# v held in two halves of 64 partitions, and another order of the instruction streams, in a packed attention with a gated convolution

## The chip, the core and the metric

The kernel runs on one core of a Trainium2 chip. TensorE (PE) multiplies matrices into PSUM; its weight loads are shown apart as PEld. VectorE (DVE), ScalarE (ACT) and GpSimd (POOL) work on tiles, and SyncE (SP) issues the DMAs. The metric is the device time of one execution in microseconds (us). All arithmetic is on 32-bit floats.

## The reference

Eight batches, eight heads, 576 tokens, 64 channels a head, 32 packed queries p a head. The packed queries attend to the tokens; then the tokens attend to the packed result. The heads side by side give x, which goes through a causal convolution of five taps for a gate, a value product and an output product.

```python
def sm_attn(qq, kk, vv):
    s = scale * np.matmul(qq, kk.transpose(0, 1, 3, 2))
    s = s - np.max(s, axis=-1, keepdims=True)
    a = np.exp(s)
    a = a / (np.sum(a, axis=-1, keepdims=True) + 1e-09)
    return np.matmul(a, vv)
p_packed = sm_attn(p, k, v)
out = sm_attn(q, p_packed, p_packed)

gate = 1.0 / (1.0 + np.exp(-gate_pre))   # gate_pre: five taps of conv_w over x
val = x @ w_val
return (gate * val @ w_out).astype(np.float32)
```

## The kernel before

The work of a batch is cut into steps, each a Python generator that yields after a few instructions. `ORDER` is a string of tokens: a letter for the step, the batch, and how many pieces of it to emit now. `run` takes the tokens in turn, and `InOrder` ties each instruction to the one before it on its engine. So the string alone sets the order on all five engines.

The letters: K, V, Q, P load k, v, q, p; L and J load the weights of the value and output products, and C, W, N turn them from 64-bit floats, which come as pairs of words, into 32-bit ones. k and q turn k and q so that channels lie on partitions: batches 0 and 1 by TensorE (`turned`, TURNED), the others by VectorE's transpose of 32x32 blocks. a is the attention of the packed queries: scores s1 into the PSUM tile `quad`, of which there is one; a maximum (nb); Exp into a1; transposes of a1 in pieces of 128 columns (at) and ScalarE copies (a1t); the product pv with v. p and c prepare the packed result. s and t are the attention of the tokens, its softmax with the sums on VectorE, and a2 with its high part a2h and its rest a2l. g is the gate, half a batch at a time, also in `quad`; w and v (the small letter) make the value product in three parts of lower precision and multiply it with the gate into gvh and gvl; o is the output product, one chunk of 128 tokens at a time, copied into one of two `osb` buffers and stored. H is an idle turn: four transposes of the identity that nobody reads.

A head's 576 tokens lie as nine to a partition (NE = 9): a partition holds tokens 9w to 9w+8 of one head. Two heads of a group of partitions share a tile, so v of a batch is two tiles of 128 partitions, 64 partitions to a head of each pair (G = 2). In `attn_pack` the transposes take, for each e of nine, the 64 columns of both groups together; pv multiplies, for each e and group, 64 rows of a1t by 64 rows of v for each of four heads.

SP issues loads in the order of the string, and a load waits until its buffer is free. k and q share five buffers ("m"), v has four.

Of the kernel before, what the change touches and what calls it, by code (L numbers as in the profile page):

```python
# [15 lines left out]


NB = {
    "words": 4, "top": 1, "vtop": 4, "p": 1, "m": 5, "a1": 1, "v": 4, "xT": 4, "pT": 1, "a1t": 1, "pp3": 1, "ppk": 1, "t2": 3, "a2h": 3, "a2l": 3,
    "wp": 3, "sig": 3,  # L20
}

# [6 lines left out]


ORDER = """
J0 L0.2 C0.4 P0 C0 K0 N0 K0 C0.2 N0.2 C0 W0 L0 W0 Q0 W0 N0 k0.7 W0 N0 W0 N0.2 W0 H0 W0.2 k0.2 Q0 k0 W0 k0 C0 k0 L0
k0 W0 q0 k0.2 W0 N0 a0.2 q0 V0 q0 W0 C0 q0 N0 a0.2 W0.2 H0 L0 V0 a0 W0.3 a0.7 q0 C0 q0 W0 J0 q0 W0 N0 a0 W0.2 N0.2
q0.3 a0 p0 N0 q0 p0 q0 W0 N0 W0 s0 N0 s0 W0 K1.2 s0.3 k1 N0 k1 P2 k1 V1 k1 Q1 k1.5 H0 k1 s0 H0 s0 t0 k1 c0 k1 q1.2
Q1 s0 q1 k2 q1 t0.2 a1 q1 H0 a1 s0 K2 J0 q1 H0 t0.3 H0.2 a1.2 q1.4 t0.3 w0 q1 k2.2 a1 q1 t0 J0 W0 t0 W0 t0 c0 a1 K3
N0.2 a1 w0.2 a1 K2 a1 g0 N0.3 k2 W0 N0.3 a1 V1 v0 g0 v0 a1 a2 Q2.2 a2 a1 N0.4 a2 a1 a2 a1 a2 K3 a2 p1 k3 p1 k3 a2 s1
N0.2 V2 N0 a2 s1 W0 | s1 V2 v0.2 V3 N0.4 v0.2 a2 k3.2 v0 g0 P4 V4 v0 g0 v0 s1 a2 v0 s1 q2 a2.2 a3.2 K4 s1 a2 t1 s1
v0 N0 V3 a3 t1 a2 p2 Q3 a3 o0 k4 k5 v0 p2 t1 o0.2 a3 q2 t1.2 s1 t1 s1 t1 k4 t1 o0 p2 o0 a3 p2 K4 v0 a3 c1 s2 a3 v0
t1 s2.3 t1.2 c1 t1 v0 a3 s2 K5 w1 g1 w1 s2 w1 g1 v1 s2 a3.2 g1 t2 v1 k4 v1 v0 k4 s2 Q3 o0 a3 v1 s2 g1 v1 a4 v1.2 k5
a3 a4 t2.3 a4.2 a3 t2 v1 o0 v1 V4 o0 q3 K5 q3 a4 p3 a4 p3 o1 v1.5 t2 o1 a4 p3.2 K6 w2 a4 o0 t2.2 k5 s3.2 Q4 c2 a4.2  # L40
t2 s3 t2 o1 w2 o1 a4 t2.2 s3 w2 P6 c2 g2 k5 g2 v2 a5 o1 v1 a4 a5 o0 a5.2 v2 a5 k6 v2 o0 s3 a4 s3 v1 Q4 v2 q4 a5 o1
V5 a5 s3 t3 a5.3 t3 a4 g2 q4 t3 V5 p4.2 t3 p4 v2 k6 K6 Q5 s3.2 p4 v2 o1 v2 g2 o0 a5 s4 a5 v2 s4 v2 s4.2 o1 v2 s4 v2
k6 V7 Q5 o2 k6 t3 a5 o2 o1 Q6 t3.2 c3.2 t3 a6 k7 o1 a5 s4 a6.3 p5 v2 k7 o1 v2 t3 o2.2 t3 q5 a6.2 K7 a6 v2 t3 v2 t3
V6 o2 w3.2 p5 s4 g3.2 w3 o1 a6 t4 s4.2 v3.4 Q6 t4.2 p5 g3 a6 p5 o2 v2 q5 g3 o2.3 q6 v3 a6 v3.2 o1 v3 t4 v3 V6 o3 v3
t4.2 o1.2 c4 v3.3 a6 k7 a6 s5 v3 s5 t4 o3.2 s5 c4 a6 o2 t4 o3 s5.2 a6 w4 o2 t4.4 w4 g4 o3 p6 w4 o3 q6 g4 p6 s5 v4 p6
v4 g4 v4 g4 K7 v4 s5 k7 V7 v3 s5 p6 v3 v4.2 t5.2 o2 t5 o3 s6.2 Q7 t5 v4 t5 v4 s6 o3 s6 v4 o3 v4 s6.3 o3 a7 s6 v4 a7
o4 v4 o3.2 t6 a7.2 t5 s5 o4 s6 v4 a7 t5 a7 Q7 o4.2 c5 t5 v4 o4 t5.2 a7 c5 t5.2 w5.2 g5 w5 a7 v5 a7 g5.2 a7 g5 v5 a7
t6.5 c6 a7 v5.3 v4 o3 v5.2 v4 v5.2 o5 v5.2 a7 o3 o4 c6 t6.2 o4 o3 a7 q7.2 v5 t6 p7 o5 p7.2 o4 v5 p7 o5 s7.2 o4 s7.2
t6 s7.3 t6 o5 v5 o4 o5 t7 t6 w6.3 g6.2 v6 g6 v5 v6.2 o5 o4 v5 v6 t7 s7 t7 s7 v6.2 t7 v6 t7.3 o5 o4 o5 v6 g6 v6 c7
v6.3 o6 v6.2 t7 o5.2 t7 o6 t7.3 o5 c7 g7.2 w7 o6 g7 w7.2 o5 g7 v7.2 v6 v7 o5.2 v7 o6.2 v7 v6 v7 o7 v7.2 o7 v7.4 o5  # L50
o6.4 v7 o7 v7.3 o7.27 o6 H0 o6.2
"""


# [25 lines left out]
def packed_attention_gated_conv(  # L80
# [8 lines left out]
    w_out: bass.AP,  # L89
    out: bass.AP,  # L90
):

# [86 lines left out]
            st["p", b + n] = t[:, n]  # L181
        yield

    def load(b, nm, src, tag="m"):
        rows = src[b].rearrange("h s d -> (h s d)").rearrange("(h a x) -> a h x", h=4, a=P)
        for n in range(2):
            m = st[nm, b, n] = tile_of(tag, [P, 2, NE, D], F32, f"{nm}m_{b}_{n}")
            sp.dma_start(m.rearrange("a h e d -> a h (e d)"), rows[:, 2 * n : 2 * n + 2])
            yield

# [1 line left out]
        yield from load(b, "k", k)  # L192

    def load_v(b):
        yield from load(b, "v", v, "v")

    def load_q(b):
        yield from load(b, "q", q)
# [140 lines left out]
    def keys(b):  # L339
        if b in TURNED["k"]:  # L340
            if b % 2 == 0:
                pd = tile_of("osb", [P, 4, 2 * D], F32, f"pd_{b}")
                act.mul(
                    pd.rearrange("a h (u d) -> a h u d", u=2),
                    st["p", b].unsqueeze(2).broadcast_to([P, 4, 2, D]),
                    scale,
                )
                yield
                pt = one(f"pTt_{b}").rearrange("a (h x) -> a h x", x=P)
                for hl in range(4):  # L350
                    pe.transpose(pt[:, hl], pd[:, hl], ident)
                yield
                pT = tile_of("pT", [P, 4, P], F32, f"pT_{b}")
                for n in range(2):
                    st["pT", b + n] = pT.rearrange("a h (g n j) -> a h g n j", g=G, n=2)[:, :, :, n]
                act.copy(pT, pt)
                yield
            yield from turned(b, "k")
            return
        t = st["p", b]  # L360
        pT = st["pT", b] = tile_of("pT", [P, 4, 2, NP], F32, f"pT_{b}")
        act.mul(t, t, scale)
        yield
        dve.transpose(pT.rearrange("a h c z -> a (h c z)"), t.rearrange("a h d -> a (h d)"))
        yield
        yield from channels(b, "k")

    def channels(b, nm):
        for n in range(2):
            xT = st[f"{nm}T", b, n] = tile_of("xT", [P, 2, NE, D], F32, f"{nm}T_{b}_{n}")  # L370
            dve.transpose(
                xT.rearrange("a h e d -> a (h e d)"),
                st[nm, b, n].rearrange("a h e d -> a (h e d)"),
            )
            yield

    def queries(b):
        if b in TURNED["q"]:
            yield from turned(b, "q")
            return  # L380
        yield from channels(b, "q")

    def scores(name, b, pT, nm):

# [14 lines left out]
    def scores_turned(name, b, pT, nm):  # L399


        s = quad(name)[:, :, :HS]
        for g in range(G):
            for par in range(2):
                rows = slice(D * par, D * par + D)
                for hl in range(4):
                    to = s[heads[hl], 2 * g + par, : 2 * P]
                    xT = st[f"{nm}T", b, hl // 2][rows, hl % 2, :NE4, NW * g : NW * g + NW]
                    pe.matmul(
                        to.rearrange("a (e w) -> a e w", w=NW), pT(g, hl)[rows], xT, start=True, stop=True  # L410
                    )
        for t in range(NQ):
            for hl in range(4):
                xT = st[f"{nm}T", b, hl // 2][:, hl % 2, NE4, NP * t : NP * t + NP]
                pe.matmul(
                    s[heads[hl], t, 2 * P : 2 * P + NP], pT(t // 2, hl), xT, start=True, stop=True
                )
        return s

    def attn_pack(b):  # L420
# [3 lines left out]
        else:  # L424
            s1 = scores(f"s1_{b}", b, lambda rows, c, hl: pT[rows, hl, c], "k")
        yield
        a1 = tile_of("a1", [P, NE, G, NW], F32, f"a1_{b}")
        parts = 2 if b in TURNED["k"] else 1
        sums = tile_of("sm1", [P, 2, G], F32, f"sm1_{b}")
        rs = sums[:, 0]  # L430
        for g in range(G):
            x = s1[:, 2 * g : 2 * g + 2]
            nb = tile_of("nb1", [P, 1], F32, f"nb1_{b}_{g}")
            dve.tensor_reduce(nb, x, axis=AX.XY, op=ALU.max, negate=True)
            yield
            if b in TURNED["k"]:
                pairs = (
                    (
                        a1[:, : 2 * NE4, g].rearrange("a (e t) w -> a t e w", t=2),
                        x[:, :, : 2 * P].rearrange("a t (e w) -> a t e w", w=NW),  # L440
                    ),
                    (a1[:, 2 * NE4, g].rearrange("a (t z) -> a t z", t=2), x[:, :, 2 * P :]),
                )
            else:
                pairs = (
                    (
                        a1[:, :, g].rearrange("a e (t z) -> a t e z", t=2),
                        x.rearrange("a t (e z) -> a t e z", z=NP),
                    ),
                )  # L450
            for n, (to, of) in enumerate(pairs):
                act.activation(to, of, AF.Exp, bias=nb, accum_out=sums[:, n, g : g + 1])
            yield
        if b in TURNED["k"]:
            dve.scalar_tensor_tensor(rs, rs, 1e-9, sums[:, 1], op0=ALU.add, op1=ALU.add)
        else:
            dve.tensor_scalar_add(rs, rs, 1e-9)
        dve.reciprocal(rs, rs)
        yield
        a1t = tile_of("a1t", [P, NE, P], F32, f"a1t_{b}")  # L460
        for n in range(0, NE, NE4):
            es = range(n, min(n + NE4, NE))
            at = one(f"at_{b}_{n}").rearrange("a (e y) -> a e y", y=P)
            for e in es:
                pe.transpose(at[:, e - n], a1[:, e].rearrange("a g w -> a (g w)"), ident)
            yield
            act.copy(a1t[:, n : n + len(es)], at[:, : len(es)])
            yield
        pv = big(f"pv_{b}")[:, :, :D]
        for e in range(NE):  # L470
            for g in range(G):
                rows = slice(NW * g, NW * g + NW)
                for hl in range(4):
                    pe.matmul(
                        pv[heads[hl], g],
                        a1t[rows, e, heads[hl]],
                        st["v", b, hl // 2][rows, hl % 2, e],
                        start=(e == 0),
                        stop=(e == NE - 1),
                    )  # L480
        yield
        if b in TURNED["q"]:
            pp3 = st["pp3", b] = tile_of("pp3", [P, G, 2, D], F32, f"pp3_{b}")
# [286 lines left out]
```

## Time and profile before

| what | us |
|---|---|
| median of 3 runs | 312.02 |
| the runs | 312.02, 314.77, 311.74 |
| the profiled execution | 315.61 |
| its span, first to last instruction | 313.8 |

All further numbers are from the profiled execution. A row of its views names the engine, the operation, what is written and from what, the tile on the array (128*32 is 128 rows by 32 columns), shapes and a count. L63 is the line of the helper that issues everything. A 32-bit product is recorded as two matmuls and two weight loads; transposes and the products of the value and output steps as one of each. Matmuls overlap, so a group's time comes from its start to the next group's, not from the time of one. The loads by tile, with the number of DMAs, KB each and the median time from issue to landing:

```profile
km<-in_k_dram SPq DMA_DIRECT2D x16, 576.0 KB, 5.2
qm<-in_q_dram SPq DMA_DIRECT2D x16, 576.0 KB, 6.5
vm<-in_v_dram SPq DMA_DIRECT2D x16, 576.0 KB, 5.8
out_dram<-osb SPq DMA_DIRECT2D x72, 128.0 KB, 2.4
```

### The profile page before, as it was taken

The page shows a single profiled execution, that of the slowest core. Times are in us where ns is not written, and L with a number is a line of the kernel's source. Part 1 is how long each engine was busy: PE and PEld are TensorE (multiplying, and loading weights), DVE is VectorE, ACT ScalarE, POOL GpSimd, SP SyncE. Part 2 cuts the span into 40 slices and gives each one's busy share as a digit, 9 for nine tenths or more (in the row PEclk, how much of TensorE's full clock was granted, in tenths as well). Part 3 has the DMA queues.
Part 4 walks back from the last instruction along what each step waited for, and adds up shares of the span by engine and source line. Part 5 has one row for each costly group of instructions (what it writes and reads, how often), then busy time and mean ns, then how long its engine had stood idle before and what let it go on. Part 6 is the DMA issues. An engine that isn't in the chain of part 4 may idle for free.

```text
span 313.8 us, 10411 instructions
## 1 busy us (share of the span) xinstructions
PE 285.8 (91%) x4652; PEld 219.1 (70%) x4652; DVE 193.4 (62%) x302; ACT 142.4 (45%) x271; POOL 77.2 (25%) x84
## 2 busy tenths in 40 slices
PE   0898888898999999799999999999999999999963
PEld 0675655576678687487778877777887678589842
DVE  1764699799997875629765646885467574223110
ACT  3555567736664346333564126365532454442011
POOL 3542930644440130205022021143210312000000
PEclk9977799999999999789999999999999999999999
DMA  7999766554934636806713206243012113111134
GB/s 233 394 392 289 264 229 197 194 179 146 308 99 131 161 91 221 303 8 153 244 40 95 65 22 206 91 97 116 0 38 69 33 36 70 37 33 36 33 87 114
DMA packets 23903, 43.55 MB, mean 139 GB/s; under 512 B 5898, under 2 KB 5938, under 8 KB 23858
## 3 DMA queue, kind: packets, MB, share of 16 engines
q1 hardware_dynamic: 23858, 42.89, 45.1%
q8 instruction: 36, 0.59, 0.8%
q14 instruction: 9, 0.07, 0.1%
HBM read 33.44 MB, written 9.44 MB: 137 GB/s over the span
## 4 chain that ended last, share of the span: by engine, by line
PE 76%; DVE 9%; ACT 5%; DMA 4%; issue 3%; SPq 1%; DVEq 0%; ACTq 0%
PE o L63 28%; PE val L63 16%; PE gate L63 13%; PE s L63 6%; PE pv L63 3%; PE at L63 2%; PE kt L63 2%; ACT a L63 2%; DVE t L63 2%; PE wp L63 2%; DVE sm L63 2%; DMA p<-in_p_dram 2%; DMA out_dram<-osb 1%; DMA km<-in_k_dram 1%; DVE nb L63 1%
## 5 line engine op out<-in xcount | busy, mean ns | idle before, releaser
L63 PE MATMUL o<-woh,gvh 128*128 128x512 f32 x144 | 57.9, 402 | 2.4 <-ACT osb L63 1.5
L63 PE MATMUL o<-wol,gvh 128*128 128x512 f32 x144 | 56.4, 392 | 0.0
L63 PE MATMUL o<-woh,gvl 128*128 128x512 f32 x144 | 56.2, 391 | 0.0
L63 PE MATMUL gate<-a,ppk 32*64 32x288 f32 x1280 | 45.8, 412 | 4.0 <-issue 2.3
L63 DVE SCALAR_TENSOR_TENSOR sig<-sig,val 128x576 f32<-128x576 f32 x32 | 24.0, 749 | 31.0 <-PE val L63 27.6
L63 PEld LDWEIGHTS gate<-a,ppk 32*64 32x64 f32 x1280 | 29.5, 133 | 19.0 <-issue 9.8
L63 PE MATMUL val<-a2h,wph 128*128 128x288 f32 x128 | 40.4, 316 | 0.1
L63 PE MATMUL val<-a2h,wpl 128*128 128x288 f32 x128 | 38.3, 300 | 0.0
L63 PE MATMUL val<-a2l,wph 128*128 128x288 f32 x128 | 38.3, 299 | 0.0
L63 ACT COPY osb<-o 128x512 f32<-128x512 f32 x34 | 19.9, 584 | 40.6 <-PE o L63 27.1
L63 ACT CAST gvh<-sig 128x576 fp32r<-128x576 f32 x32 | 21.4, 672 | 32.6 <-DVE sig L63 32.6
L63 POOL TENSOR_TENSOR t<-t,sm 128x576 f32<-128x576 f32 x14 | 16.6, 1182 | 77.9 <-DVE sm L63 56.2
L63 PEld LDWEIGHTS o<-woh,gvh 128*128 128x128 f32 x144 | 27.2, 189 | 10.6 <-ACT osb L63 2.4
L63 PEld LDWEIGHTS o<-woh,gvl 128*128 128x128 f32 x144 | 27.2, 189 | 6.0
L63 PEld LDWEIGHTS o<-wol,gvh 128*128 128x128 f32 x144 | 27.2, 189 | 4.6
L63 DVE TENSOR_TENSOR gvl<-sig,gvh 128x576 fp32r<-128x576 f32 x32 | 25.1, 788 | 8.6 <-ACT gvh L63 8.3
L63 PEld LDWEIGHTS val<-a2h,wph 128*128 128x128 f32 x128 | 24.6, 192 | 7.5 <-DVE wpl L63 3.1
L63 POOL TENSOR_TENSOR t<-t,mx 128x576 f32<-128x576 f32 x14 | 16.7, 1192 | 52.9 <-DVE mx L63 52.8
L63 ACT ACTIVATE sig<-gate 128x1152 f32<-128x1152 f32 x16 | 18.2, 1134 | 18.4 <-PE gate L63 18.4
L63 PEld LDWEIGHTS val<-a2h,wpl 128*128 128x128 f32 x128 | 24.6, 192 | 0.4
L63 PEld LDWEIGHTS val<-a2l,wph 128*128 128x128 f32 x128 | 24.6, 192 | 0.0
L63 DVE TENSOR_REDUCE nb<-s 128x1 f32<-128x576 f32 x16 | 11.9, 746 | 12.2 <-ACT a L63 6.2
(97 smaller groups left out, 438.6 us busy)
## 6 DMA issues: line engine op xcount, KB each, us to landing
km<-in_k_dram SPq DMA_DIRECT2D x16, 576.0 KB, 5.2
qm<-in_q_dram SPq DMA_DIRECT2D x16, 576.0 KB, 6.5
vm<-in_v_dram SPq DMA_DIRECT2D x16, 576.0 KB, 5.8
out_dram<-osb SPq DMA_DIRECT2D x72, 128.0 KB, 2.4
wo_words<-in_moe_w_out_dram SPq DMA_DIRECT2D x4, 512.0 KB, 7.2
wv_words<-in_moe_w_val_dram SPq DMA_DIRECT2D x4, 512.0 KB, 8.4
p<-in_p_dram SPq DMA_DIRECT2D x12, 64.0 KB, 3.6
p<-in_p_dram SPq DMA_DIRECT2D x4, 32.0 KB, 5.2
```

The source lines that it names most:

```text
L63: made = getattr(self.engine, op)(*args, **kw)
```

## The change

v. Eight of a partition's nine tokens now lie in a tile of 128 partitions: the first four of all eight heads on partitions 0 to 63, the next four on 64 to 127. The ninth tokens go to a tile of their own on 64 partitions, of which there is one. A batch is loaded by three DMAs (512, 512 and 128 KB) instead of two of 576 KB, in runs of 1024 and 256 bytes instead of 2304.

a1. A group's 576 columns are now kept together, so a transpose of 128 columns gives 128 rows of one group that match v's two halves. There are four such transposes a group and one of 64 columns for the ninth tokens, ten in all instead of nine, and pv is 2 x 4 x 4 products of 128 rows and 2 x 4 of 64, 40 instead of 72. In batches 0 and 1 one Exp covers all 288 columns of both halves, where there were two, and the scores write the odd tokens at the head of the second half. In the other batches the order of tokens in a1 comes from k: its transpose by VectorE is two instructions, one of eight tokens that interleaves the halves and one for the ninth. Outside these steps no arithmetic is changed.

```diff
-            m = st[nm, b, n] = tile_of(tag, [P, 2, NE, D], F32, f"{nm}m_{b}_{n}")
...
     def load_v(b):
-        yield from load(b, "v", v, "v")
+        rows = v[b].rearrange("h (w e) d -> w h (e d)", e=NE)
+        m = st["v", b] = tile_of("v", [P, H, NE4, D], F32, f"vm_{b}")
+        for o in range(2):
+            sp.dma_start(
+                m[NW * o : NW * o + NW].rearrange("a h i d -> a h (i d)"),
+                rows[:, :, NE4 * D * o : NE4 * D * (o + 1)],
+            )
+            yield
+        m = st["v9", b] = tile_of("v9", [NW, H, D], F32, f"v9_{b}")
+        sp.dma_start(m, rows[:, :, 2 * NE4 * D :])
+        yield
...
             dve.transpose(
-                xT.rearrange("a h e d -> a (h e d)"),
-                st[nm, b, n].rearrange("a h e d -> a (h e d)"),
-            )
+                xT[:, :, : 2 * NE4].rearrange("a h (i o) d -> a h o i d", o=2),
+                m[:, :, : 2 * NE4].rearrange("a h (o i) d -> a h o i d", o=2),
+            )
+            dve.transpose(xT[:, :, 2 * NE4], m[:, :, 2 * NE4])
...
-        a1 = tile_of("a1", [P, NE, G, NW], F32, f"a1_{b}")
+        a1 = tile_of("a1", [P, G, S], F32, f"a1_{b}")
...
-            for n, (to, of) in enumerate(pairs):
-                act.activation(to, of, AF.Exp, bias=nb, accum_out=sums[:, n, g : g + 1])
+            act.activation(to, x, AF.Exp, bias=nb, accum_out=rs[:, g : g + 1])
...
-                pe.transpose(at[:, e - n], a1[:, e].rearrange("a g w -> a (g w)"), ident)
+        for g in range(G):
+            at = one(f"at_{b}_{g}").rearrange("a (i y) -> a i y", y=P)
+            for i in range(NE4):
+                x = first[i]
+                pe.transpose(at[:, i], a1[:, g, x : x + P], ident)
+            yield
+            act.copy(a1t[:, g], at)
+            yield
+        at = one(f"at_{b}_9")[:NW, : G * P].rearrange("a (g y) -> a g y", y=P)
...
+        for g in range(G):
+            for i in range(NE4):
                 for hl in range(4):
                     pe.matmul(
                         pv[heads[hl], g],
-                        a1t[rows, e, heads[hl]],
-                        st["v", b, hl // 2][rows, hl % 2, e],
+                        a1t[:, g, i, heads[hl]],
+                        st["v", b][:, 2 * hl + g, i, :],
...
-J0 L0.2 C0.4 P0 C0 K0 N0 K0 C0.2 N0.2 C0 W0 L0 W0 Q0 W0 N0 k0.7 W0 N0 W0 N0.2 W0 H0 W0.2 k0.2 Q0 k0 W0 k0 C0 k0 L0
+H0 J0 L0 H0 C0.5 N0.5 C0.2 P0 K0 k0 L0 k0.2 K0 k0.3 H0 k0 C0 Q0 k0.2 N0.2 k0.3 W0 k0 q0 k0.2 L0 q0 a0 q0 W0 C0 W0.3
```

The whole of `ORDER` is another string with the same steps and nine idle turns. Where it changes the start of SP's queue (wo, wv and cw are weights; vm and v_0 are v and its ninth tokens), before:

```order
L63 DMA wo_words<-in_moe_w_out_dram 128x1024
L63 DMA cw_words<-in_moe_conv_w_dram 40x128
L63 DMA wv_words<-in_moe_w_val_dram 128x1024
L63 DMA p_96<-in_p_dram 32x4x64 x4
L63 DMA km_0_102<-in_k_dram 128x2x576
L63 DMA km_1_106<-in_k_dram 128x2x576
```

and now:

```order
L63 DMA wo_words<-in_moe_w_out_dram 128x1024
L63 DMA cw_words<-in_moe_conv_w_dram 40x128
L63 DMA p_113<-in_p_dram 32x4x64 x4
L63 DMA km_0_118<-in_k_dram 128x2x576
L63 DMA wv_words<-in_moe_w_val_dram 128x1024
L63 DMA km_1_131<-in_k_dram 128x2x576
```

The first load of the value weights went behind p and the first half of k. On TensorE the program began with the transposes of p and k, before:

```order
L63 MATMUL pTt_124<-ident,pd_122 128x128 x4
L63 MATMUL kt_0_0_132<-ident,km_0_102 128x128 x4
L63 MATMUL kt_0_1_138<-ident,km_0_102 128x128 x4
L63 MATMUL idle_150<-ident 128x128 x4
L63 MATMUL kt_0_9_158<-ident,km_0_102 64x128 x2
```

and now:

```order
L63 MATMUL idle_84<-ident 128x128 x4
L63 MATMUL idle_93<-ident 128x128 x4
L63 MATMUL pTt_124<-ident,pd_120 128x128 x4
L63 MATMUL kt_0_0_134<-ident,km_0_118 128x128 x4
L63 MATMUL kt_0_1_140<-ident,km_0_118 128x128 x4
```

Two idle turns went to the very front. In batch 4, where the profile of before has its third pause, TensorE had the end of pv, two groups of transposes and the second gate in a row (a row is one product of the program, which is recorded as two):

```order
L63 MATMUL pv_1948<-vm_0_1054,a1t_1710 32x64 x2
L63 MATMUL pv_1948<-vm_1_1661,a1t_1710 32x64 x2
L63 MATMUL at_0_2035<-ident,a_5_1920 128x128 x4
L63 MATMUL at_4_2047<-ident,a_5_1920 128x128 x4
L63 MATMUL gate_1_2056<-a_0_75,ppk_1780 64x288 x40
L63 MATMUL ppTt_2107<-ident,pp_4_2102 128x128 x2
```

and now has the first gate, the last transposes, pv and the scores of batch 5, of which the first rows are:

```order
L63 MATMUL o_3_1679<-woh,gvl 128x512
L63 MATMUL at_1_1712<-ident,a_4_1458 128x128 x4
L63 MATMUL gate_0_1719<-a_0_75,ppk_1614 64x288 x40
L63 MATMUL at_9_1761<-ident,a_4_1458 64x128 x2
L63 MATMUL pv_1773<-vm_1581,a1t_1618 32x64 x32
L63 MATMUL pv_1773<-v_4_1597,a1t_4_1619 32x64 x8
L63 MATMUL s_5_1825<-kT_0_1578,pT_1207 32x288 x2
L63 MATMUL s_5_1825<-kT_1_1674,pT_1207 32x288 x2
```

The second gate went behind an output chunk and a value chunk of 12 products each. On VectorE, behind the transpose of the last weights a_0 ahead of the first gate, stood before:

```order
L63 STREAM_TRANSPOSE a_0_75<-t_0_1_457 128x64
L63 STREAM_TRANSPOSE pT_542<-p_470 128x256
L63 STREAM_TRANSPOSE kT_0_665<-km_0_594 128x1152
L63 TENSOR_TENSOR a2l_1_676<-a_0_75,a2h_1_671 128x576
L63 SCALAR_TENSOR_TENSOR sm_1_590<-sm_1_590 128x2
```

and now:

```order
L63 STREAM_TRANSPOSE a_0_75<-t_0_1_448 128x64
L63 TENSOR_SCALAR wo_words<-wo_words 128x512
L63 STREAM_TRANSPOSE pT_544<-p_450 128x256
L63 SCALAR_TENSOR_TENSOR wo_top<-wo_top,wo_words 128x512
L63 STREAM_TRANSPOSE kT_0_624<-km_0_433 128x2x2x4x64
L63 STREAM_TRANSPOSE kT_0_624<-km_0_433 128x2x64
L63 STREAM_TRANSPOSE kT_1_628<-km_1_604 128x2x2x4x64
```

Steps of the second output weight (wo_words, wo_top) came behind it, and k's transposes are two instructions each.

## What the change was predicted to do

> **What bounds the kernel now.** I read first the page's head, then TensorE's work by stretch of the program, then the chain that ended last.
>
> ```profile
> span 313.8 us, 10411 instructions
> PE 285.8 (91%) x4652; PEld 219.1 (70%) x4652; DVE 193.4 (62%) x302; ACT 142.4 (45%) x271; POOL 77.2 (25%) x84
> ...
> PEclk9977799999999999789999999999999999999999
> ...
> q8 instruction: 36, 0.59, 0.8%
> ```
>
> TensorE works for 91% of the span, the others far less. The clock dips near the start and at about 130 us. Instructions come over a DMA queue of their own: 36 packets of 16 KB, and 2 x 4652 instructions of TensorE over 36 are 258 to a packet. The windows give each stretch as start and end, its length, the busy time of PE, PEld, DVE, ACT and POOL, the clock, the DMA share and GB/s.
>
> ```profile
> 9.00:49.00 40.00, 35.21 (x526) 25.66 (x526) 27.49 (x48) 23.05 (x55) 20.89 (x23) 0.87 0.89 302
> 49.00:94.00 45.00, 41.11 (x1002) 31.02 (x1001) 42.23 (x68) 28.38 (x53) 18.55 (x16) 1.00 0.59 189
> 94.00:122.00 28.00, 27.77 (x528) 21.28 (x528) 19.71 (x30) 11.86 (x24) 3.98 (x4) 1.00 0.45 122
> 122.00:137.00 15.00, 12.39 (x255) 9.50 (x254) 8.58 (x16) 6.49 (x14) 2.27 (x2) 0.77 0.66 251
> 137.00:290.00 153.00, 152.73 (x2277) 119.03 (x2277) 89.75 (x132) 65.94 (x114) 28.84 (x27) 1.00 0.29 76
> ```
>
> The span has four parts. Up to 49 us a chain of loads, transposes and softmax steps leads to the first gate. From 49 to 94 us VectorE is busy 42.2 of 45 us and sets the pace. From 94 to 290 us TensorE does, but for the 15 us around 130. The end is a chain of output copies and stores. The chain of waits names single pieces (start, length, what):
>
> ```profile
> 3.45 4.77 DMA p<-in_p_dram
> ...
> 30.20 2.39 issue
> ...
> 70.99 1.29 issue
> ...
> 127.56 2.28 issue
> 129.84 2.21 PE gate L63 x28
> 132.05 0.83 PE ppTt L63 x3
> 132.88 2.88 PE val L63 x12
> 135.76 3.06 PE o L63 x12
> ...
> 192.14 0.33 PE ppTt L63 x3
> 192.47 2.61 PE gate L63 x80
> 195.08 1.78 PE val L63 x12
> 196.85 2.75 PE o L63 x12
> ```
>
> "issue" is TensorE standing still with no wait for another engine. Each such pause follows a run of short instructions while the DMA engines are full:
>
> ```profile
> 30.00:32.00 2.00, 0.20 (x23) 0.08 (x11) 0.00 (x0) 0.00 (x0) 1.86 (x3) 1.00 1.03 352
> ...
> 126.00:128.00 2.00, 1.56 (x44) 0.76 (x29) 1.93 (x7) 0.20 (x1) 0.00 (x0) 1.00 1.07 396
> ```
>
> I read them as an instruction packet queued behind data while a dense part uses up the packet before it. After the third pause the clock is half, and the same work costs more: gate 2.21 instead of 28/80 of 2.61 = 0.91, ppTt 0.83 instead of 0.33, val 2.88 instead of 1.78, o 3.06 instead of 2.75, together 3.2 us.
>
> **The change part by part.** The product pv and its transposes:
>
> ```profile
> 179.38 1.70 PE L63 MATMUL pv<-vm,a1t 64*32 64x64 f32 x144
> ...
> 155.38 0.44 PE at L63 x4
> ...
> 16.44 0.35 PEld L63 LDWEIGHTS s<-kT,pT 128*32 128x32 f32 x32 [0.41 <-issue]
> ```
>
> Before, a batch has 72 products of 64 rows, recorded as 144. Now it has 32 of 128 rows and 8 of 64, recorded as 80. Tiles of 128 rows by 32 columns run four side by side instead of eight. The gate streams 288 columns in eight tiles at 2.61 us / 80 = 32.6 ns a record, which is 261 ns for one tile, so 64 columns take 58 ns, over four tiles 14.5 ns; 80 of them take 1.16 us. The lower bound is the pace of pv now, 1.70/144 = 11.8 ns, giving 0.94 us; the upper is no overlap at all, 80 x 58 ns = 4.6 us. The nearest row, scores' odd tokens in the same tile shape, loads 32 in 0.35 us, 11 ns each, so I stay by 1.16: 0.5 us less a batch. Ten transposes instead of nine cost 0.44/4 = 0.11 us more; bounds 0 and 0.2.
>
> The early chain, up to the first gate:
>
> ```profile
> 1.64 0.36 SPq L63 DMA_DIRECT2D wv_words<-in_moe_w_val_dram  x1
> ...
> 18.68 0.32 ACT L63 ACTIVATE a<-s,nb 128x64 f32<-128x64 f32 x1
> 18.88 0.21 ACT L63 ACTIVATION_READ_ACCUMULATOR a<-s,nb 128x1 f32 x1
> ...
> 8.00:16.00 8.00, 6.79 (x56) 5.32 (x64) 5.88 (x12) 4.91 (x10) 4.47 (x5) 1.00 1.04 396
> ...
> 304.00:312.00 8.00, 4.86 (x22) 3.79 (x22) 0.69 (x1) 1.26 (x3) 0.00 (x0) 1.00 0.60 141
> ```
>
> One weight load is issued behind p and the first k now, no longer ahead of p. It holds 512 KB, at 396 GB/s 1.3 us, and its issue 0.36; I take 1.2 us off the start (bounds 0.36 and 1.7). Two idle turns go ahead of everything, into time in which TensorE has nothing. The softmax of batch 0 loses one ACTIVATE and one read of its accumulator for each of two groups, 2 x 0.53 = 1.0 us, and all of it lies on the chain. The extra transpose and a copy of 256 instead of 128 columns give back 0.4. The pause at 30.2 (2.39) ends in front of the last products of the scores, and VectorE waits for those. In the new order 160 instructions of pv stand there instead of 288, so I count the pause as gone: in all -1.2 -1.0 +0.4 -2.4 = -4.2 us at the first gate.
>
> From there VectorE sets the pace, so what it gets more is lost again:
>
> ```profile
> 27.66 0.68 DVE L63 SCALAR_TENSOR_TENSOR wo_top<-wo_top,wo_words 128x512 uint32<-128x512 uint32 x1
> ...
> 28.86 0.43 DVE L63 TENSOR_SCALAR wo_words<-wo_top 128x512 uint32<-128x512 uint32 x1
> ...
> L63 DVE STREAM_TRANSPOSE kT<-km 128x1152 f32<-128x1152 f32 x12 | 16.2, 1359 | 0.4 <-DMA km<-in_k_dram 0.4
> ...
> L63 DVE STREAM_TRANSPOSE t<-s 128x576 f32<-128x576 f32 x16 | 11.7, 758 | 9.2 <-PE s L63 9.2
> ...
> L63 DVE TENSOR_TENSOR gvl<-sig,gvh 128x576 fp32r<-128x576 f32 x32 | 25.1, 788 | 8.6 <-ACT gvh L63 8.3
> ```
>
> Two steps of an output weight, 1.1 us, ran at 28 us in VectorE's free time and stand behind the gate now. The transpose of k falls into one of 1024 and one of 128 columns; 576 cost 758 ns and 1152 1359, so 1.04 ns a column and 0.16 us a start, hence 0.16 us more for each of six (bounds 0 and 0.3, as the new pattern has one more dimension): 1.0. One gvl step (0.7 with overlap) goes behind the stretch. Sum +1.4, so this stretch ends 2.8 us earlier than before. The pause at 71.0 falls into it; VectorE covers its loss, and I count nothing.
>
> Where TensorE is the bound, five batches of pv save 5 x 0.5 = 2.5, five transposes cost 0.55, and an idle turn that came after all other work stands between two gates now.
>
> ```profile
> L63 PE MATMUL idle<-ident 128*128 128x128 f32 x36 | 6.1, 312 | 0.5 <-ACT qT L63 0.5
> ```
>
> Nine turns took 6.1 us, so one costs 0.7. That makes -1.2. The third pause and its half clock are 2.3 + 3.2 = 5.5 us on the path. There pv, transposes and gate made 288 + 16 + 104 instructions in a row up to the pause; now a gate of 160, pv of 160 and scores of 128 follow each other, and the other gate comes after an output chunk and a value chunk, 24 long instructions each. I count it as gone. Loads of v in halves are hidden there: the DMA share is 0.29 to 0.66. The stores at the end keep their order and their two buffers.
>
> ```profile
> 299.91 0.59 ACT osb L63
> ...
> 309.39 0.58 ACT osb L63
> ```
>
> These 9.5 us from the first to the last output copy stay. Sum: -2.8 -1.2 -5.5 = -9.5 us on the span of 313.8, that is 304.3, or 306.1 on the profiled execution's 315.61. The median of the runs, 312.02, lies 3.6 us below that execution, and one of the three runs (314.77) 2.8 above it. The half clock costs about as much, so it may be missing from the two faster runs. I take half of it, 1.6, off the gain: 312.0 - 7.9 = 304.1 us.
>
> **The rivals.** The first is that the pauses come back. Nothing in the change moves less data, and the densest place now, scores and pv of batches 4 and 3 (128 + 160 instructions, 1.53 + 1.16 us), is followed by slow ones but may meet a burst of loads. For it speaks that all pauses lie under a full DMA; against it, that 416 instructions of scores and pv in a row at 145 us passed without one (the window from 137 to 290 us has 0.3 us of idle time in all). If all come back, 2.4 + 2.3 + 1.6 are lost again: 310.4. The Trainium skill's page "Runtime: NRT & Kernel Launch", section "Instruction fetch mechanics", says that crossing a 16 KiB block costs one DMA tail-bump and is mostly hidden. By that rule no order would gain on fetches, and the time would be this rival's 310.4; the three "issue" rows do not agree with it.
>
> The second is that v in halves and VectorE eat the early gain. Stores from 64 partitions moved 141 GB/s at a share of 0.60, which is 235 at a full one, while loads to 128 moved 396. At that rate v's 1.18 MB take 5.0 us instead of 3.0, and in the first 33 us the DMA is full, so the next q and k come 2 us later. With the +1.4 at its upper bound the 2.8 are gone: 306.9. The Trainium skill's page "DMA: Bandwidth & Descriptors", section "Rules for kernel authors", advises against two transfers to disjoint partition halves, which it says serialize, and for one over 128 partitions. By it the sum would be 2.0 higher, 306.1.
>
> The third is slower: the four column tiles of a 128-row product do not overlap, because the weights of the next are loaded only when the one before is done. Then a batch's pv takes 4.6 us instead of 1.7; five batches make +14.5 in place of -2.5, and the time is 321. From 34 ns a record on (14.5 plus 7.9 us over 400 records) the change is no gain. The row of 11 ns speaks against it, but those had 32 columns and few in a row.
>
> **How the numbers follow.** My forecast 304.1 has a chance of 0.55, the pauses 0.18, the eaten gain 0.17, the serial tiles 0.10. The range leaves out the last. It reaches up past the pauses to 311. Down, pv at its lower bound (-1), a start at its bound (-0.5), and the whole half clock (-1.6) with 2 us of waits in the new order that go unseen make 299. Within 1%, about what a measurement here can tell from no change, is 308.9 to 315.1. Faster: 0.50 of the first, 0.05 of the second, 0.12 of the third case, 0.67. Same: 0.05 + 0.13 + 0.05 = 0.23. Slower: the third, 0.10.
>
> **What would show it.** Right: pv at 1.0 to 1.3 us with 80 records; about 32 instruction packets; no "issue" piece over 1 us after 94 us, and a clock of 1.00 from there; the first gate at about 44 to 46 us; VectorE over 90% busy until s of batch 4. Wrong: a pause behind scores and pv near 92 us, a clock below 1.00 after 94 us, pv over 2 us, TensorE waiting for q or k at 20 to 30 us.

## The result, and the profile after

The changed kernel took 317.51 us, the median of 20 runs (314.26 to 325.44), and the kernel before 313.77 (20 runs, 310.45 to 315.05). The ratio is 1.011, with a 95% interval of 1.0075 to 1.0146: about 1% slower, where 304.1 had been forecast and 299 to 311 as range. Six of the changed kernel's runs took 321 to 325 us, its profiled execution (324.35) is one of them, and this ratio, like all that follow, leaves out such slow runs of a kernel while the medians hold all of them; in the profile the losses are thus larger than in the median.

The page of the changed kernel:

```profile
span 322.6 us, 9430 instructions
...
PE 290.8 (90%) x4148; PEld 220.2 (68%) x4148; DVE 195.0 (60%) x314; ACT 142.0 (44%) x263; POOL 79.6 (25%) x84
...
PEclk9978999586999999599999999999999999999998
...
q1 hardware_dynamic: 32178, 42.89, 52.9%
q8 instruction: 32, 0.52, 0.8%
```

TensorE has 504 recorded matmuls fewer and is nevertheless busy 5.0 us longer: its clock is down from 56 to 80 us and near 130, besides the dip from about 16 to 32 us that both kernels have. The instruction packets are 32, as forecast. The data are the same 42.89 MB, but on the page of before they were 23858 packets and a share of 45.1%:

```profile
q1 hardware_dynamic: 23858, 42.89, 45.1%
```

The chain of waits of the changed kernel (start, length, what) has the places:

```profile
46.59 0.62 PE gate L63 x2
...
51.72 1.53 PE s L63 x55
53.26 3.60 issue
56.86 1.13 PE s L63 x8
57.99 2.45 PE pv L63 x80
...
67.52 1.37 PE pv L63 x75
68.89 3.20 issue
72.09 0.43 PE pv L63 x5
72.52 5.03 PE gate L63 x80
...
104.37 1.39 PE pv L63 x80
...
125.57 0.57 PE pv L63 x28
126.14 3.06 issue
129.20 1.86 PE pv L63 x52
```

The pause of before at 30 us is gone. Three others stand there, each longer than any of before, and work behind them is at half speed: a gate of 5.03 us instead of 2.61, a pv of 2.45 instead of 1.39. By the ends of the same steps in the two traces, the changed kernel was 4.0 us ahead at the scores of batch 1, 2.7 ahead at the first gate, 10.6 behind at the second gate of batch 0, 9.9 behind at the second gate of batch 2, and 8.8 behind at the end. So the loss arose between 53 and 78 us; at 126 us the changed kernel lost about what the other lost at 128.

The windows (start and end, length, busy time of PE, PEld, DVE, ACT, POOL, clock, DMA share, GB/s) show what the DMA engines did there, first before, then after:

```profile
48.00:56.00 8.00, 6.77 (x156) 4.94 (x161) 7.90 (x14) 6.05 (x11) 0.28 (x1) 1.00 0.73 243
60.00:76.00 16.00, 14.69 (x396) 11.14 (x397) 15.81 (x25) 8.54 (x18) 7.60 (x7) 1.00 0.49 154
117.00:128.00 11.00, 10.23 (x288) 7.35 (x287) 6.94 (x14) 6.32 (x14) 0.00 (x0) 1.00 0.74 246
```

```profile
48.00:56.00 8.00, 4.74 (x140) 3.03 (x128) 4.87 (x9) 5.40 (x9) 4.16 (x5) 1.00 0.93 167
60.00:76.00 16.00, 12.51 (x251) 8.85 (x251) 12.72 (x23) 6.65 (x15) 6.31 (x6) 0.71 0.96 260
117.00:128.00 11.00, 8.48 (x163) 5.80 (x142) 8.97 (x12) 5.41 (x9) 1.23 (x2) 1.00 0.97 245
```

The DMA engines are full at all three places. From 48 to 56 us they are full and move only 167 GB/s: those are loads of v. From 60 to 76 us they move much more than before. The queue of SyncE shows why so much falls into that time (start, time of the issues, what):

```profile
37.68 6.81 SPq L63 DMA_DIRECT2D vm<-in_v_dram  x2
60.49 0.59 SPq L63 DMA_DIRECT2D v<-in_v_dram  x1
61.20 0.56 SPq L63 DMA_DIRECT2D wo_words<-in_moe_w_out_dram  x1
61.81 0.94 SPq L63 DMA_DIRECT2D qm<-in_q_dram  x2
62.79 0.48 SPq L63 DMA_DIRECT2D km<-in_k_dram  x1
```

Nothing is issued from 44.5 to 60.5 us. The ninth tokens of batch 2 wait for their one buffer, which pv of batch 1 holds until 60.4, and behind them stand the last output weight, q, k, v and p. They all go out from 60.5 to 69.4 us and are under way when TensorE comes to pv of batch 2, at 67.5, and to the second gate, at 72.4.

### The profile page after: what moved, and what is told of

It reads as the page before. It is cut to its first block, busy times and chain, and to the rows that moved or that the text cites. A ratio compares the mean times of both kernels' runs of the same rounds, so it can differ in the third digit from the quotient of the medians.

```text
span 322.6 us, 9430 instructions
## 1 busy us (share of the span) xinstructions
PE 290.8 (90%) x4148; PEld 220.2 (68%) x4148; DVE 195.0 (60%) x314; ACT 142.0 (44%) x263; POOL 79.6 (25%) x84
## 3 DMA queue, kind: packets, MB, share of 16 engines
q1 hardware_dynamic: 32178, 42.89, 52.9%
## 4 chain that ended last, share of the span: by engine, by line
PE 72%; DVE 8%; issue 7%; DMA 6%; ACT 3%; SPq 2%; ACTq 0%; DVEq 0%
PE o L63 26%; PE val L63 16%; PE gate L63 14%; PE s L63 6%; DMA vm<-in_v_dram 5%; PE pv L63 5%; DVE t L63 2%; SPq L63 2%; PE wp L63 2%; PE at L63 2%; DMA out_dram<-osb 1%; DVE sig L63 1%; PE ppTt L63 1%; DVE qT L63 1%; DVE sm L63 1%
## 5 line engine op out<-in xcount | busy, mean ns | idle before, releaser
L63 DVE TENSOR_TENSOR gvl<-sig,gvh 128x576 fp32r<-128x576 f32 x32 | 27.1, 849 | 16.4 <-ACT gvh L63 16.2
L63 POOL TENSOR_TENSOR t<-t,mx 128x576 f32<-128x576 f32 x14 | 18.0, 1288 | 58.4 <-DVE mx L63 58.3
L63 ACT ACTIVATE a<-s,nb 128x576 f32<-128x576 f32 x16 | 11.9, 742 | 18.5 <-DVE nb L63 18.5
```

Of the source, the lines that this page charges most:

```text
L63: made = getattr(self.engine, op)(*args, **kw)
```

## The experiments

The median of the kernel before lay at 313.1 to 314.0 us beside all of these. Ratios are to it, with the 95% interval.

**Layout and order apart.** The first run has the new layout under the order of before, the second the new order with the old layout (loads, transposes and pv are those of before). Only the tokens for v are fitted to the number of loads, in each batch as in these:

```diff
-H0 L0 V0 a0
+H0 L0 V0.2 a0
```

```diff
-a1 V1.2 a2
+a1 V1 a2
```

> The new layout of v and a1 (loads in halves of 64 partitions, 40 products, two transposes of k per half) under the order of before; only the third load of a batch is added behind the second. Theory D (the loads of v in halves are slow, keep the DMA full for longer, and so delay other loads and the instruction packets): most of the loss is here, 2 to 8 us over the kernel before (314 to 321), packets of 1024 bytes at about 90 ns, pauses of TensorE over 2 us under a full DMA. Theory O (the new order is what costs): the layout alone gains 0.3 us per batch of pv, 308 to 312.

> The new order with the layout, loads and products of before; the third token of each load of v is left out. Theory D: the pauses in the first 130 us shrink to those of before or fewer, 304 to 310. Theory O: as slow as the changed kernel or slower, since it has the longer pv as well: 317 to 323.

| kernel | us | ratio |
|---|---|---|
| layout alone | 312.35 | 0.991 (0.987 to 0.995) |
| order alone | 324.63 | 1.027 (1.020 to 1.034) |

Both expectations of theory D fell; theory O named the right sides, with figures a little low. The layout alone is a small gain, though its halves of v landed nearly as slowly (8.2 us after issue in the median), and its only pause is of 0.6 us. The order alone is the worst. So the layout is worth 5 to 7 us under the new order, slow loads and all, and 2 to 3 under the old one. The windows of the order alone:

```profile
48.00:56.00 8.00, 7.35 (x295) 5.19 (x295) 5.84 (x9) 6.18 (x11) 3.93 (x5) 0.90 0.02 4
60.00:76.00 16.00, 10.13 (x287) 6.68 (x272) 11.05 (x13) 5.90 (x12) 8.74 (x7) 0.81 0.84 261
```

There the last output weight held the queue until 55.5 us, since it waited for VectorE's steps on the weight ahead of it, which free the buffer: 4 GB/s for 8 us, then 261 under the dense part. So the order bunches the loads by itself, without any load of v in halves.

**What the pauses are.** Small transposes of the identity ahead of everything shift the packet boundaries, while the order and the DMAs stay. In `idle_turns`:

```diff
+        pt = one("shift")
+        for _ in range(64):
+            pe.transpose(pt[:NP, :NP], ident[:NP, :NP], ident[:NP, :NP])
```

> The changed kernel with 64 transposes of 32x32 of the identity ahead of everything, in time in which TensorE waits for p; they are 128 instructions (loads and products), half an instruction packet, so every packet boundary falls 128 instructions earlier in the program while order and DMAs stay. Theory F (the pauses are packets that come late): the pause in the scores of batch 2 goes, the one in pv of batch 2 moves back to the gate of batch 0 or goes, the one in pv of batch 4 moves forward to the gate of batch 2 ahead of it. Theory P (a pause belongs to that place in the program, such as to its DMA burst or its dense part alone): the three stay where they were, in s of batch 2, pv of batch 2 and pv of batch 4, and the time stays at 315 to 319. Under F the time is 311 to 317.

> The same with 96 transposes, 192 instructions. By the starts of instructions in the changed kernel's trace the packets then have 6 to 9 us where they needed 4 to 9. Theory F: pauses of at most about 1.5 us, at other places than before, 308 to 314. Theory P: three pauses of over 3 us at the old places, 315 to 320.

They took 320.62 us (1.021, 1.014 to 1.029) and 323.35 (1.023, 1.013 to 1.034). The chain of the first, at two places:

```profile
60.40 1.39 PE pv L63 x80
61.79 2.11 PE gate L63 x59
63.90 2.73 issue
...
122.18 0.70 PE s L63 x11
122.88 3.61 issue
```

and of the second:

```profile
62.42 1.39 PE pv L63 x80
63.81 1.14 PE gate L63 x27
64.94 1.49 issue
...
120.98 1.02 PE pv L63 x60
122.00 5.30 issue
```

In the changed kernel these pauses came after 75 recorded matmuls of pv of batch 2 and 28 of pv of batch 4. In the first run they come 5 + 59 = 64 and 52 + 11 = 63 matmuls later, which with their weight loads is half a packet; in the second 5 + 27 = 32 and 60 - 28 = 32 later, a quarter. A boundary that stands 128 or 192 of 256 instructions earlier means that the next one stands 128 or 64 later, and there TensorE stops. Theory P is refuted: a pause is a packet boundary. The times of theory F failed, though: neither of the other two phases was cheaper. Between 63 and 69 us and between 122 and 127 a boundary met a burst in all three. The pause in the scores of batch 2 shrank to 1.15 us in the first run, as expected, but the one at batch 4 went the other way than I had said.

The old layout in the new order, shifted by 128, went the same way:

> The new order with the layout of before, shifted by 128 instructions. If the new order lost because of where its packet boundaries fell: three or more of the five pauses go or shrink, 313 to 320. If the new order is worse by itself: 322 to 327.

332.38 us (1.057, 1.048 to 1.065), worse than the 324.63 unshifted and above both of my branches. The order's loss is no bad luck with one phase.

**The loads of v.** All of these keep the changed kernel's order. One loads v to 128 partitions at a time, which puts v's tokens out of their places; two cut the two loads into eight, by turns (the second diff) or with the loops over `h` and `o` exchanged:

```diff
+        flat = v[b].rearrange("h s d -> (h s d)").rearrange("(a y x) -> a y x", a=P, y=4)
         for o in range(2):
             sp.dma_start(
-                m[NW * o : NW * o + NW].rearrange("a h i d -> a h (i d)"),
-                rows[:, :, NE4 * D * o : NE4 * D * (o + 1)],
+                m[:, 4 * o : 4 * o + 4].rearrange("a h i d -> a h (i d)"),
+                flat[:, :, NE4 * D * o : NE4 * D * (o + 1)],
             )
```

```diff
-        for o in range(2):
-            sp.dma_start(
-                m[NW * o : NW * o + NW].rearrange("a h i d -> a h (i d)"),
-                rows[:, :, NE4 * D * o : NE4 * D * (o + 1)],
-            )
-            yield
+        for h in range(0, H, 2):
+            for o in range(2):
+                sp.dma_start(
+                    m[NW * o : NW * o + NW, h : h + 2].rearrange("a h i d -> a h (i d)"),
+                    rows[:, h : h + 2, NE4 * D * o : NE4 * D * (o + 1)],
+                )
+            if h % 4 == 2:
+                yield
```

> The changed kernel, but the two large loads of v each go to all 128 partitions and four heads, in the same runs of 1024 bytes and the same number of descriptors; v's tokens are then not in their places, so the output is not attention over v as it stands. Theory D by partitions (half of the partitions is what makes it slow): 1024-byte packets at about 46 ns, a batch of v in 3 us, fewer or shorter pauses, 303 to 309. Theory D by run length (1024 bytes instead of 2304 is what makes it slow): packets stay near 90 ns, 316 to 319. Theory O: 316 to 319 whatever the packets take.

> The changed kernel with v loaded in eight pieces of two heads, first half and second half by turns, so that both halves are in flight together; the data are right. Theory D by partitions: packets faster than 90 ns, nearer to 46, 305 to 312, less what six more issues of about 0.5 us on SyncE cost. By run length, or if the pieces do not overlap: 316 to 320.

> The changed kernel with v in the same eight pieces of two heads as in the run with turns, but the first half's four ahead of the second half's four. Theory D by partitions (it is the turns that let both halves move together): packets of 1024 bytes near 90 ns and 315 to 318. Theory S (small pieces, each with its own issue of about 0.5 us on SyncE, leave less queued ahead of an instruction packet, and the turns do nothing): 308 to 311 as with turns.

| loads of v | us | ratio |
|---|---|---|
| two, each to 64 partitions (the change) | 317.51 | 1.011 (1.008 to 1.015) |
| two, each to 128 partitions | 311.32 | 0.993 (0.988 to 0.997) |
| eight, halves by turns | 308.77 | 0.987 (0.982 to 0.991) |
| eight, one half after the other | 309.73 | 0.988 (0.983 to 0.994) |

The issues of v with their sizes and the median time to landing, for the changed kernel, the load to 128 partitions, and the eight pieces one half after the other:

```profile
vm<-in_v_dram SPq DMA_DIRECT2D x16, 512.0 KB, 9.0
```

```profile
vm<-in_v_dram SPq DMA_DIRECT2D x16, 512.0 KB, 6.5
```

```profile
vm<-in_v_dram SPq DMA_DIRECT2D x64, 128.0 KB, 6.1
```

With 128 partitions the packets of 1024 bytes took 46 ns in the median, with 64 they took 87. The packets came out as theory D by partitions said, the time a little above its 303 to 309. So it is the half of the partitions, not the short run, that makes v slow, and that costs 6 us in this order. The Trainium skill's page "DMA: Bandwidth & Descriptors", section "Rules for kernel authors", prefers one transfer over all partitions to two on disjoint halves; this pair agrees. The pieces give more still, without turns too (78 ns a packet), so the turns that I had thought of as the cause are not needed. The page of that run has the same program on TensorE, with far less time:

```profile
PE 280.2 (92%) x4148; PEld 214.0 (70%) x4148; DVE 194.4 (63%) x314; ACT 141.6 (46%) x263; POOL 79.8 (26%) x84
```

That is 10.6 us less busy than in the changed kernel's profile, which I read as work at half clock: the mean granted clock was 0.99 here and 0.95 there. The pauses are 3.4 us instead of 10.5. I also worked out from the trace's records how late a packet starts, counted from the place in TensorE's stream, one in every 256 instructions, at which it starts when the DMA is idle. The three longest times were 5.2, 4.4 and 4.3 us before, 8.8, 7.6 and 7.3 in the changed kernel, 7.7, 4.7 and 4.6 with 128 partitions, and 4.4, 4.3 and 4.2 with the eight pieces.

TensorE stops when it has used up the next 256 instructions before the packet has started, landed and been taken up; from the packet's start to TensorE's next instruction it was 2.5 to 2.8 us at the three pauses. There and at the same instructions with the eight pieces one half after the other, the records give (us):

| place | changed kernel: wait | 256 used up in | pieces: wait | 256 used up in |
|---|---|---|---|---|
| scores of batch 2 | 6.3 | 4.8 | 1.5 | 4.8 |
| pv of batch 2 | 4.5 | 3.9 | 2.9 | 4.4 |
| pv of batch 4 | 8.8 | 8.2 | 3.4 | 7.9 |

The program uses up its packets about as fast in both; what the pieces change is the wait.

**SyncE's queue.** Two tokens, three loads, are moved, so that q and k go out ahead of the load that waits:

```diff
-V2 s1 a2 V2 N0 a2.4 N0.2 a2 k3 V2 a2 J0 N0.2 s1 N0 g0 N0 a2 s1 p2 Q2.2 K3 q2
+V2 s1 a2 V2 Q2.2 K3 N0 a2.4 N0.2 a2 k3 V2 a2 J0 N0.2 s1 N0 g0 N0 a2 s1 p2 q2
```

> The changed kernel with three tokens moved: the loads of q and of the second half of k that stand behind the ninth tokens of batch 2 and the last output weight go ahead of them on SyncE's queue. In the changed kernel the queue stands from 44.5 to 60.5 us, since the buffer of the ninth tokens is not free, and then issues eight loads in 8 us. Theory Q (the queue stands behind a load that waits for its buffer, and the loads behind it then meet the dense part of TensorE): the pause in pv of batch 2 (3.2 us) and the half clock after it go or shrink, 3 to 6 us less than the changed kernel, 311 to 314. If the bytes alone make the burst, wherever they are issued: 316 to 319.

> The changed kernel with both mends, v in eight pieces by turns and q and k ahead of the ninth tokens. If the two are separate costs: 1 to 3 us less than with the turns alone, 306 to 308. If the turns had already taken what the queue cost: 308 to 310.

315.07 us (0.998, 0.994 to 1.003), and 311.75 (0.994, 0.991 to 0.998) with the pieces. The first is a gain on the changed kernel of 0.8% by the medians and 1.3% by the ratios, short of theory Q's 311 to 314: the pause of 3.20 us is gone, but others of 1.35 and 1.06 and stretches of half clock stay. With the pieces the same edit loses 3 us, where I had expected a gain or nothing. So the standing queue seems to be a small part of the cause, and unblocking it is no mend of its own.

**Smaller loads in general.** In `load`, for k and q (and v in the old layout):

```diff
-            sp.dma_start(m.rearrange("a h e d -> a h (e d)"), rows[:, 2 * n : 2 * n + 2])
+            for j in range(2):
+                sp.dma_start(m[:, j].rearrange("a e d -> a (e d)"), rows[:, 2 * n + j])
```

> The kernel before with every load of 576 KB of k, q and v as two of 288 KB, one head of each pair; same bytes, same runs of 2304 bytes, twice the issues. Theory S (smaller pieces leave less ahead of an instruction packet): the pauses at 30, 71 and 128 us shrink, 309 to 312. Otherwise no change, 312 to 315.

> The new order with the layout of before (324.6 us), its loads of k, q and v in twice as many pieces of 288 KB. If the new order loses by packets that wait behind large loads: the five pauses shrink and it falls by at least 8 us, 310 to 316. If it loses for another reason, such as its idle turn or the work of VectorE behind the gate: by no more than the kernel before gained from the same edit (4.5 us), 319 to 324.

> The order of before, the new layout, and v loaded in eight pieces with the halves by turns. If the two gains add up: 1.5 to 4 us less than the layout alone with v in two loads, 308 to 311 (beside 312.35 there). If the loads of v are hidden in that order: no difference, 311 to 313.

> The order of before, the new layout with v in eight pieces by turns, and k and q in pieces of 288 KB. If the gains of small loads and of the shorter pv add up: 305 to 308. If the pauses were already gone at 308.6: 308 to 310, since the new pieces only add issues on SyncE.

> The changed kernel with v in eight pieces by turns and k and q in pieces of 288 KB. Two pauses of 1.6 and 1.3 us were left at 308.8; if pieces of k and q take them away: 305 to 308. Otherwise 308 to 310.

| kernel | us | ratio |
|---|---|---|
| before, loads halved | 309.38 | 0.987 (0.982 to 0.992) |
| order alone, loads halved | 324.60 | 1.037 (1.032 to 1.042) |
| old order, new layout, v in eight | 308.57 | 0.985 (0.979 to 0.991) |
| the same, k and q halved too | 308.04 | 0.983 (0.978 to 0.988) |
| changed kernel, v in eight, k and q halved | 311.22 | 0.989 (0.984 to 0.994) |

The kernel before gains 1.3% from the edit alone. TensorE's waits in its profile:

```profile
PE gate L63 <- issue: 2.8, 1, 2.8
PE s L63 <- issue: 0.7, 1, 0.7
```

The pause at 71 us is gone and the one at 30 small; the third stays. The order alone gains nothing; its pause in pv of batch 2 is still 3.8 us, as the queue stands there until 55.8 us whatever the size of the loads behind. The best version is the old order with the new layout and all loads small, 308.04, which beats both kernels; it can't be told from the next two. There the new order is worth nothing: 308.6 with the old order, 308.8 with the new. Halving k and q as well did not help the new order: 311.22 is above both of my branches, though the intervals of the two ratios (0.989 and 0.987) overlap.

**Fewer loads.** `load_v` gives every batch the v of batch 0 (in the changed layout with `st["v9", b]` as well):

```diff
+        if b:
+            for n in range(2):
+                st["v", b, n] = st["v", 0, n]
+                yield
+            return
```

> The kernel before without the loads of v of batches 1 to 7; all batches use the v of batch 0, so 8.3 MB less are moved and the output of those batches is not attention over their v. If packets late behind loads are what its pauses cost: the three pauses shrink, 306 to 310. If not: 312 to 315.

> The new order with the layout of before, with the same loads of v left out. If the order's own loss (10.6 us) is packets that are late behind bursts of loads: its pauses near 60 to 70 and 125 us go, and it stands within 3 us of the kernel before without those loads, 307 to 313. If the order loses for another reason: still 8 us or more above that kernel, 316 to 322.

> The changed kernel with the same loads of v left out. If nothing but late packets and the loads of v stand between it and the forecast: no pause over 1.5 us and the clock at 1.00 from 49 us on, 302 to 307. If something else eats the gain: 309 or more.

308.52 us (0.983, 0.975 to 0.991), 321.00 (1.019, 1.008 to 1.030), and 310.83 (0.989, 0.982 to 0.997). The first is as expected. The other two fell into the second branches: with a quarter of the bytes read gone the new order still loses 12.5 us to the old one. So bytes alone are not what it loses by. The changed kernel without these loads still has a pause of 2.05 us in pv of batch 2 with half clock behind it, and stands 2.3 us above the kernel before without them, which the intervals do not separate, and not below it. The new layout is worth 9 to 10 us under the new order there (321.00 to 310.83 by the medians), although SyncE's queue stands until 54 us in that run as well. Its shorter pv, with 504 recorded matmuls fewer, would fit, since TensorE then uses up fewer packets; no run separates that from the rest of the layout. TensorE's time on the page of the kernel before without those loads, and of the order alone without them:

```profile
PE 280.4 (92%) x4652; PEld 215.3 (71%) x4652; DVE 193.0 (64%) x302; ACT 142.2 (47%) x271; POOL 77.2 (25%) x84
```

```profile
PE 288.0 (91%) x4652; PEld 219.7 (69%) x4652; DVE 194.6 (61%) x302; ACT 141.6 (45%) x271; POOL 79.6 (25%) x84
```

The spans are 303.8 and 317.2, 13.4 us apart. TensorE is busy 7.6 us longer for the same work, at a mean clock of 0.96 against 0.99, and pauses 6.8 us longer (7.9 against 1.1). The two cover all of it, so it is the same loss by the same two items. The longest pause of the order alone without these loads, 3.31 us in pv of batch 2, comes under the q, k and p that go out from 56 to 63 us, after SyncE has issued a single load, the last output weight at 56, since 36. That they are what is left of the burst is read from the trace; no run took them away.

## Why the prediction was wrong

**The early chain** was about right in its sum: the scores of batch 1 came 4.0 us earlier, where 4.2 were forecast for the first gate, and the pause at 30 us was gone. No run takes its terms apart. That gate itself began only 2.0 us earlier, as TensorE's view by tile says, first for before, then after:

```profile
L63 PE MATMUL gate<-a,ppk x1280: 401/401/737, 48.5 to 273.7; 32*64 32x288 f32 x183
```

```profile
L63 PE MATMUL gate<-a,ppk x1280: 400/401/735, 46.5 to 284.3; 32*64 32x288 f32 x183
```

**pv** costs 1.39 us, 17.4 ns a record, not 14.5: a saving of 0.31 a batch against 0.5. The mechanism held, four column tiles do overlap, and the third rival is out.

**VectorE's stretch** was no longer that. The forecast was over 90% busy until the scores of batch 4; it was 32.3 of 45 us, since TensorE stood still or ran at half clock:

```profile
49.00:94.00 45.00, 37.36 (x672) 26.12 (x664) 32.33 (x57) 22.18 (x46) 19.43 (x17) 0.85 0.64 164
```

**The step that failed** is "I count it as gone", for the third pause, with its twin, that the pause at 71 is covered and costs nothing. I had the mechanism, a packet queued behind data, and judged it by the instructions that follow each other alone. That side held for the third pause: the 256 instructions ahead of it were used up in 3.6 us before and in 8.2 after. The other side, how long the data keep the packet waiting, I took over from before, and it went from 3.9 us there to 8.8, so the pause stayed, at 3.06 us. The two pauses between 53 and 78 us, 3.60 and 3.20 with half clock behind them, have no term in the sum: from the end of the first gate to the end of the second the changed kernel lost 13.3 us (2.7 ahead to 10.6 behind), where 1.4 had been allowed for the whole stretch up to 94 us. What I had in hand for it, I put elsewhere: "Loads of v in halves are hidden there" was argued from DMA shares of 0.29 to 0.66 of before, while the halves and the bunching made them 0.93 to 0.97 at the three places. The half clock was priced at 3.2 us; by TensorE's busy time it cost some 10.6 in this profile, against 5.4 before (285.8 less the 280.4 of the kernel before without most v).

**Two rivals were each half right.** The pauses did come back, but the first rival took them at their old size and stopped at 310.4. v in halves was slow (1024 bytes in 87 ns on 16 engines is 188 GB/s, less than the 235 that I took), but the second rival charged it 2 us at the start, not what it does to the instruction packets. Neither price could leave the range, and the first one's size was enough to: the order alone, with no v in halves, took 324.63. The Trainium skill's page "Runtime: NRT & Kernel Launch", section "Instruction fetch mechanics", by whose "mostly hidden" no order would gain or lose on fetches, does not agree with these runs.

**What was never priced** is the order by itself: 2.7% lost, the largest single effect here. I counted its idle turn and VectorE's weight steps, but not that these steps free a buffer for which SyncE's next load waits, nor what is queued behind that load.

**Open.** Even without the loads of v of seven batches the changed kernel took 310.83, not 304.1; what keeps it from the forecast there is not known beyond the pause of 2.05 us. Why the eight pieces of v without turns shorten the packets' wait so much is not settled; that each has an issue of its own, which leaves less queued at a time, fits, but the kernel before with halved loads still had two waits of over 6 us. Nor is it settled why moving q and k ahead helps the changed kernel and hurts it once v is in pieces.

## What to carry to other kernels

When an order is changed, follow each queue that issues loads: a load that waits for its buffer holds all loads behind it, and they come out together, possibly under the densest part of the program. Judge an instruction stream of short products by both sides, how fast it uses up a packet and how full the DMA engines are when it asks for the next; cutting large loads in pieces was worth 1.3% to the kernel before, with nothing else touched. Load to all partitions where one can, and price a pause with the half clock behind it.

## What the hardware showed that was not expected

- Pauses follow packet boundaries to the instruction: with 128 and 192 instructions added in front, two of them moved by 64 and 63, and by 32 and 32 recorded matmuls.
- The granted clock was full or half and nothing between, and until the end of the span it was half for 3.41, 6.83 or 10.24 us at a time. In the changed kernel it was 6.83 us from 57.0, 70.6 and 128.7 us on, within 1.5 us of the end of each of the three pauses.
- The low clock behind the pauses costs as much as the pauses. Over the whole span of the changed kernel the pauses were 10.5 us, and TensorE was busy 10.6 us longer than in the kernel with v in eight pieces.
- Loads to 64 partitions began fast: in the changed kernel the first 100 packets of 1024 bytes of a burst took 46 to 49 ns each in the median, those after the 300th 86 to 93 in seven of eight bursts.
